# An SSM scan beside a SwiGLU block: the last feature tile's column halves in one stretch, and a layernorm moved ahead

## The chip, the cores and the metric

The kernel runs on one core of a Trainium2 chip. The metric is the device time of one execution in microseconds (us). The engines are called by their names: TensorE (PE in the profile; its weight loads are PEld), VectorE (DVE), ScalarE (ACT), GpSimd (POOL) and SyncE (SP), whose queue starts most of the DMAs.

## The reference, cut to what matters

The input x has 2048 rows (tokens) of 512 columns in bfloat16. The weights of the SwiGLU block have 1376 features. The output is the sum of x, a diagonal state space model and the SwiGLU block, both on the layernorm of x:

```python
xn = layernorm(x)                               # over the 512 columns
# state space model: 512 complex states, a recurrence over the 2048 tokens
h_t = Lam_bar * h_(t-1) + B_bar @ xn_t
y   = 2 * real(C @ h_t) + xn * Dskip
# SwiGLU
f   = (silu(xn @ w_gate) * (xn @ w_up)) @ w_down
out = x + y + f
```

## The kernel before

**Chunks.** The tokens are cut into four chunks of 512, and each chunk into four tiles of 128. `xnT` holds the transposed layernorm of all chunks. For a chunk c three stages run on TensorE: `gateup_chunk(c)` makes the products with `w_gate` and `w_up`, `bproj_chunk(c)` makes those with B (L357), and `out_chunk(c)` makes the output. `out_chunk(c)` first runs `out_ffn` for its four tiles: for each, one PSUM bank is opened and the contractions with `w_down` over the feature tiles are added into it (L513). It then runs `out_ssm` for the four tiles, which adds eight contractions of the scanned states with the matrix CF (L522) and closes the bank. The bank leaves through ScalarE (L529) and a DMA of GpSimd's queue that adds to the output in DRAM (L530); for the last chunk it leaves through VectorE. A PSUM bank holds 128x512 floats, and there are eight.

**Order of the stages.** TensorE runs, after a hand-written head: the gate of chunk 0 in two parts with bproj(0) between them, bproj(1), gate(1), bproj(2), out(0), gate(2), bproj(3), out(1), gate(3), out(2), out(3). Instructions are issued on each engine in the order in which the program's text emits them.

**The features.** 1376 features make ten tiles of 128 and a last one of 96. The gate stage begins with the last one. Its 96 gate columns and the last 32 of its up columns are put side by side into one weight tile `w_last`, so one group of four matmuls serves both (L458). The 64 up columns that are left (`wu_last`, L468) are half a weight tile. For two chunks they run as pairs of halves, 128x64 each, into the two halves of one bank's partitions. Chunks 0 and 1 have theirs in gate(1), and chunks 2 and 3 have theirs in gate(3). The results are copied by ScalarE into `ul` (L471) and multiplied by VectorE into `gu_last` (L473), of which there are two, one for even and one for odd chunks. `out_ffn` reads `gu_last` in its eleventh contraction.

**The backlog.** The work of VectorE for the state space model stands in a list, `backlog`, of entries with a cost and a tag. `pump(us)` lets as many of them out as the TensorE time that was just issued pays for; `need(tag)` lets everything out up to the last entry of that tag; `multiply(keep)` lets out the products of the gate stage (L451, L473), which stand in a list of their own. For a chunk the entries are: six rotation steps on `u` (L367, L377, L381), eight scans (L399), the carry (L408 to L413), six rotation steps back into `wt`. CF itself is made by eight entries (tag "cf"): ScalarE scales a column block into `cm` (L340, three buffers) and VectorE combines it (L343).

**The layernorms.** Those of chunks 2 and 3 go through the backlog too. `ln_rest` gives four statistics (L185, L186), the variance (L194) with GpSimd's power for the reciprocal root (L195), one VectorE entry for the bias (`nb`, L198), and four entries that normalize a tile on ScalarE (L208) and start its transposing DMA on SP's queue (L234). `spread` puts a list of entries one by one between those of another. Chunk 2's layernorm stands among chunk 0's scans; chunk 3's stands among chunk 1's scans. SP's queue also starts one DMA that copies x into the output (L734), before which no accumulating DMA may run.

Of the kernel before, what the change touches and what calls it, by code (L numbers as in the profile page):

```python
# [11 lines left out]
BF16 = mybir.dt.bfloat16  # L12
ALU = mybir.AluOpType
ACT = mybir.ActivationFunctionType
# [9 lines left out]
def kernel(  # L24
# [17 lines left out]
    nc = tc.nc  # L42
    _, L, D = A_x.shape
# [3 lines left out]
    CW = 512  # L47
    HW = CW // 2
    NT = L // 128
    NCH = L // CW  # L50
    TPC = CW // 128
    KD = D // 128
    NQ = Pst // 128
    FT = (F + 127) // 128
# [4 lines left out]
    LA, LB = 32, 64  # L59
# [4 lines left out]
    const = ctx.enter_context(tc.tile_pool(name="const", bufs=1))  # L64
    ssm = ctx.enter_context(tc.tile_pool(name="ssm", bufs=1))
    gut = ctx.enter_context(tc.tile_pool(name="gut", bufs=2))
    up_p = ctx.enter_context(tc.tile_pool(name="up_p", bufs=4))
    opool = ctx.enter_context(tc.tile_pool(name="opool", bufs=6))
# [4 lines left out]
    def bank(shape=(128, CW), dtype=F32):  # L73
        return psum.tile(list(shape), dtype, name="ps")
# [5 lines left out]
    out_v = out[0].rearrange("(n p) d -> p n d", p=128)  # L80
# [5 lines left out]
    xnT = const.tile([128, KD, L], BF16, name="xnT")  # L86
# [8 lines left out]
    wu_last = const.tile([128, KD, LB], BF16, name="wu_last")  # L95
    wd_sb = const.tile([128, FT, D], BF16, name="wd_sb")
# [5 lines left out]
    CF = const.tile([128, 2, NQ, D], BF16, name="CF")  # L102
# [62 lines left out]

    gu_last = [const.tile([128, CW], BF16, name=f"gu_last{i}") for i in range(2)]
    for t in (gu_last[0][LB + LA:128, :], gu_last[1][LB + LA:128, :], wd_sb[LB + LA:128, FT - 1, :]):
        nc.vector.memset(t, 0.0)  # L170


# [11 lines left out]
    def ln_stats(n):  # L184
        nc.vector.bn_stats(out=stats[:, n, :], in_=xall[:, n, :])  # L185
        nc.vector.bn_aggr(out=mv[:, n, :], in_=stats[:, n, :])  # L186
# [6 lines left out]
    def ln_rstd(a, b):  # L193
        nc.vector.tensor_scalar(out=ve[:, a:b], in0=mv[:, a:b, 1], scalar1=EPS, scalar2=None, op0=ALU.add)  # L194
        nc.gpsimd.tensor_tensor(out=rstd[:, a:b], in0=ve[:, a:b], in1=neg_half[:, 0:b - a], op=ALU.pow)  # L195

    def ln_nb(a, b):
        nc.vector.scalar_tensor_tensor(out=nb[:, a:b], in0=mv[:, a:b, 0], scalar=-1.0, in1=rstd[:, a:b],  # L198
                                       op0=ALU.mult, op1=ALU.mult)
# [32 lines left out]
    def xT_dma(n):  # L232
        c, i = divmod(n, TPC)
        nc.sync.dma_start_transpose(out=xnT[:, :, n * 128:(n + 1) * 128], in_=xn_tile(c)[:, i, :])  # L234
# [12 lines left out]
    V = nc.vector  # L247
# [177 lines left out]
    gu_tiles = {}  # L425
    u_pair = {}
    products = []
# [24 lines left out]

    up_last = {}

    def gateup_last(c):
        ps = bank()
        for k in range(KD):
            nc.tensor.matmul(ps[:], lhsT=w_last[:, k, :], rhs=xnT[:, k, c * CW:(c + 1) * CW],  # L458
                             start=(k == 0), stop=(k == KD - 1))
        u = up_last[c] = up_p.tile([128, CW], BF16, name="ul", bufs=2)  # L460
        nc.scalar.activation(out=gu_last[c % 2][0:LB + LA, :], in_=ps[0:LB + LA], func=ACT.Silu)
        nc.scalar.copy(out=u[LB:LB + LA, :], in_=ps[LB + LA:128])
        if c % 2 == 0:
            return
        ps = bank()
        for k in range(KD):
            for i in range(2):
                nc.tensor.matmul(ps[i * LB:(i + 1) * LB], lhsT=wu_last[:, k, :],  # L468
                                 rhs=xnT[:, k, (c - 1 + i) * CW:(c + i) * CW], start=(k == 0), stop=(k == KD - 1))
        for i in range(2):  # L470
            nc.scalar.copy(out=up_last[c - 1 + i][0:LB, :], in_=ps[i * LB:(i + 1) * LB])  # L471
            g, u = gu_last[(c - 1 + i) % 2][0:LB + LA, :], up_last[c - 1 + i][0:LB + LA, :]
            products.append(lambda g=g, u=u: V.tensor_tensor(out=g, in0=g, in1=u, op=ALU.mult))  # L473

    def gateup_tile(c, fi):
        if fi == FT - 1:
# [22 lines left out]
    o_tiles = {}  # L499

    def out_blocks(n):

        return ((0, D // 2), (D // 2, D - 128), (D - 128, D)) if n == NT - 1 else ((0, D),)

    def out_ffn(n):
        c, i = divmod(n, TPC)
        o_tiles[n] = []
        for lo, hi in out_blocks(n):
            o = bank((128, hi - lo))
            o_tiles[n].append(o)  # L510
            for fi in range(FT):
                t = gu_last[c % 2] if fi == FT - 1 else gu_tiles[c][:, fi, :]
                nc.tensor.matmul(o[:], lhsT=t[:, i * 128:(i + 1) * 128], rhs=wd_sb[:, fi, lo:hi],  # L513
                                 start=(fi == 0), stop=False)

    def out_ssm(n):
        c, i = divmod(n, TPC)
        res = opool.tile([128, D], BF16, name="res")
        for o, (lo, hi) in zip(o_tiles[n], out_blocks(n)):
            for part in range(2):  # L520
                for q in range(NQ):
                    nc.tensor.matmul(o[:], lhsT=w_tiles[c][:, part, q, i * 128:(i + 1) * 128],  # L522
                                     rhs=CF[:, part, q, lo:hi], start=False, stop=(part == 1 and q == NQ - 1))
            if c == NCH - 1:
                V.tensor_tensor(out=res[:, lo:hi], in0=o[:], in1=xn_end[:, i, lo:hi], op=ALU.add)  # L525
                for a, b in ((0, D // 2), (D // 2, D)) if i == 0 else ((lo, hi),):
                    (nc.sync if b == D else nc.scalar).dma_start(out=out_v[:, n, a:b], in_=res[:, a:b])
            else:
                nc.scalar.copy(out=res[:, lo:hi], in_=o[:])  # L529
                nc.gpsimd.dma_start(out=out_v[:, n, lo:hi], in_=res[:, lo:hi], accum_op=ALU.add)  # L530

# [4 lines left out]
    def queue(tag, ops, at=None):  # L538
        ops = [[op[0], op[1], op[2] if len(op) > 2 else None, tag] for op in ops]
        if at is None:  # L540
            backlog.extend(ops)
        else:
            backlog[at:at] = ops

    def step():
        for item in backlog[0:AHEAD + 1]:
            if item[2] is not None:
                item[2]()
                item[2] = None
        cost, op, _, _ = backlog.pop(0)  # L550
        op()
        owed[0] -= cost

    def pump(us):

        owed[0] += us
        while backlog and owed[0] >= backlog[0][0] * 0.5:
            step()
        if not backlog:
            owed[0] = 0.0  # L560

    def multiply(keep):

        while len(products) > keep:
            products.pop(0)()
            owed[0] -= 0.65

    def need(tag):

        while any(item[3] == tag for item in backlog):  # L570
            step()
# [12 lines left out]
    def ln_rest(c, on_act):  # L584
        ops = [(0.7, lambda n=n: ln_stats(n)) for n in range(c * TPC, (c + 1) * TPC)]
        def fin():
            ln_rstd(c * TPC, (c + 1) * TPC)
        def nbf():
            ln_nb(c * TPC, (c + 1) * TPC)
        ops += [(0.1, fin)]  # L590
        tail = [(0.1, nbf)] if on_act else []
        for n in range(c * TPC, (c + 1) * TPC):
            def one(n=n):
                (norm_act if on_act else norm_dve)(n)
                xT_dma(n)
            tail.append((0.05 if on_act else 0.35, one))
        return ops, tail
# [70 lines left out]
    def gateup_chunk(c):  # L668
        for fi in [FT - 1, *range(FT - 1)]:
            gateup_tile(c, fi)  # L670
            pump(GU)
            multiply(1)

    def out_chunk(c):

        multiply(0)
        for n in range(c * TPC, (c + 1) * TPC):
            out_ffn(n)
            pump(FT * 0.2163)
        need(f"ssm{c}")  # L680
        need("cf")
        for n in range(c * TPC, (c + 1) * TPC):
            out_ssm(n)
            pump(2 * NQ * 0.2163)

    def spread(ops, others, tag, tag2):

        others = list(others)
        for op in ops:
            queue(tag, [op])  # L690
            if others:
                queue(tag2, [others.pop(0)])

    def queue_ssm(c):
        fwd, back = ssm_ops(c)
# [12 lines left out]
    fwd0, back0 = ssm_ops(0)  # L708
    stats2, norm2 = ln_rest(2, True)
    queue("ssm0", fwd0[0:2] + [(1.5, params_b)] + fwd0[2:6])  # L710
    queue("ln2", stats2)
    queue("ssm0", fwd0[6:8])
    spread(fwd0[8:] + back0, norm2, "ssm0", "ln2")
    queue("cf", c_ops())
    load_late()
    for fi in range(G0, FT):
# [6 lines left out]

    bproj_chunk(1)
    fwd1, back1 = ssm_ops(1)
    stats3, norm3 = ln_rest(3, True)
    queue("ssm1", fwd1[0:6])
    queue("ln3", stats3)
    queue("ssm1", fwd1[6:8])
    spread(fwd1[8:] + back1, norm3, "ssm1", "ln3")  # L730
    gateup_chunk(1)
    nc.gpsimd.dma_start(out=dsk_bc[:], in_=A_Dskip.partition_broadcast(128))
    bproj_chunk(2)
# [44 lines left out]
```

## Time and profile before

| what | value |
|---|---|
| time, median of 3 runs | 179.62 us (179.45 to 179.9) |
| the profiled execution's own time | 179.41 us |
| its span in the profile | 177.6 us |
| TensorE busy | 172.7 us |
| VectorE busy | 154.2 us |
| ScalarE busy | 94.3 us |
| DMA traffic | 15.53 MB |
| granted TensorE clock | 1.0 |

The span runs from the first to the last instruction that the profile has; the execution's own time is 1.8 us longer. In a row of the timeline stand the start in us from the span's start, the duration in us, the engine, the line, the operation, the tiles and shapes, the number of instructions that were merged into the row, and in brackets the engine's idle time just before, with what ended it. Matmuls are pipelined: the duration of one is longer than the distance between the starts of two.

### The profile page before, as it was taken

The page shows a single profiled execution, that of the slowest core. Times are in us where ns is not written, and L with a number is a line of the kernel's source. Part 1 is how long each engine was busy: PE and PEld are TensorE (multiplying, and loading weights), DVE is VectorE, ACT ScalarE, POOL GpSimd, SP SyncE. Part 2 cuts the span into 40 slices and gives each one's busy share as a digit, 9 for nine tenths or more (in the row PEclk, how much of TensorE's full clock was granted, in tenths as well). Part 3 has the DMA queues.
Part 4 walks back from the last instruction along what each step waited for, and adds up shares of the span by engine and source line. Part 5 has one row for each costly group of instructions (what it writes and reads, how often), then busy time and mean ns, then how long its engine had stood idle before and what let it go on. Part 6 is the DMA issues. An engine that isn't in the chain of part 4 may idle for free.

```text
span 177.6 us, 2450 instructions
## 1 busy us (share of the span) xinstructions
PE 172.7 (97%) x900; PEld 83.1 (47%) x916; DVE 154.2 (87%) x237; ACT 94.3 (53%) x173; POOL 23.2 (13%) x29
## 2 busy tenths in 40 slices
PE   8999999999999999999999999999999999999993
PEld 2784444444444444444444444444444444444743
DVE  6789997999999999999999999999999999940033
ACT  4589696978499965033997660024866600220000
POOL 6003000001300000029000000013505000150000
PEclk9999999999999999999999999999999999999999
DMA  5998948993146400022820000007276900072012
GB/s 157 320 265 234 146 95 232 350 140 89 30 87 208 181 0 0 0 30 29 122 61 0 0 0 0 4 2 85 30 119 94 147 0 0 0 87 32 4 49 69
DMA packets 29131, 15.53 MB, mean 87 GB/s; under 512 B 18848, under 2 KB 29056, under 8 KB 29088
## 3 DMA queue, kind: packets, MB, share of 16 engines
q1 hardware_dynamic: 24416, 11.41, 28.3%
q0 software_dynamic: 3456, 3.28, 13.9%
q10 hardware_dynamic: 1248, 0.69, 1.4%
q8 instruction: 7, 0.11, 0.3%
q14 instruction: 4, 0.03, 0.1%
HBM read 8.03 MB, written 5.24 MB: 75 GB/s over the span
## 4 chain that ended last, share of the span: by engine, by line
PE 95%; DVE 1%; DMA 1%; issue 1%
PE ps L432 36%; PE ps L513 21%; PE ps L357 15%; PE ps L522 15%; PE ps L605 3%; PE ps L458 2%; DMA xall<-in_A_x_dram 1%; PE ps L468 1%; PE ps L220 1%; DVE stats L185 0%; DVE stats L612 0%; DVE xall L203 0%; DVE res L525 0%; PE ps L582 0%; DVE mv L186 0%
## 5 line engine op out<-in xcount | busy, mean ns | idle before, releaser
L432 PE MATMUL ps<-xnT,wg 128*128 128x512 bf16 x143 | 37.6, 379 | 0.3
L432 PE MATMUL ps<-xnT,wu 128*128 128x512 bf16 x146 | 37.5, 379 | 0.1
L513 PE MATMUL ps<-wd_sb,guT 128*128 128x512 bf16 (+2 forms) x177 | 37.2, 355 | 0.2
L399 DVE TENSOR_TENSOR_SCAN g<-r_t,car,u 128x512 bf16<-128x512 f32 x24 | 28.9, 1266 | 0.0
L522 PE MATMUL ps<-CF,wt 128*128 128x512 bf16 (+2 forms) x140 | 28.1, 355 | 0.2
L357 PE MATMUL ps<-xnT,BT 128*128 128x512 bf16 x126 | 28.2, 379 | 0.1
L529 ACT CAST res<-ps 128x512 bf16<-128x512 f32 x12 | 7.0, 585 | 38.4 <-PE ps L522 38.4
L446 ACT ACTIVATE guT<-ps 128x512 bf16<-128x512 f32 x40 | 24.8, 620 | 3.8 <-PE ps L432 3.7
L447 ACT CAST u<-ps 128x512 bf16<-128x512 f32 x40 | 24.2, 604 | 4.1 <-PE ps L432 4.0
L513 PEld LDWEIGHTS <-guT 128*128 128x128 bf16 x180 | 16.9, 98 | 18.0
L432 PEld LDWEIGHTS <-wu 128*128 128x128 bf16 x148 | 14.5, 98 | 17.5
L432 PEld LDWEIGHTS <-wg 128*128 128x128 bf16 x148 | 14.3, 98 | 17.6 <-issue 0.8
L530 POOL DMA_DIRECT2D out_dram<-res x12 | 11.1, 998 | 87.2 <-ACT res L529 87.2
L522 PEld LDWEIGHTS <-wt 128*128 128x128 bf16 x144 | 13.5, 98 | 14.2
L357 PEld LDWEIGHTS <-BT 128*128 128x128 bf16 x128 | 12.5, 98 | 15.1
L359 ACT CAST u<-ps 128x512 bf16<-128x512 f32 x32 | 17.5, 589 | 3.1 <-PE ps L357 3.0
L525 DVE TENSOR_TENSOR res<-ps,xn_end 128x512 bf16<-128x512 f32 (+2 forms) x6 | 3.0, 514 | 14.5 <-PE ps L522 14.5
L451 DVE TENSOR_TENSOR guT<-guT,u 128x1024 bf16<-128x1024 bf16 x20 | 13.5, 680 | 0.0
L367 DVE TENSOR_TENSOR pm<-u,c 128x2048 bf16<-128x2048 bf16 x8 | 9.8, 1221 | 1.2 <-ACT c L284 1.1
L195 POOL TENSOR_TENSOR rstd<-ve,neg_half 128x4 f32<-128x4 f32 x3 | 5.2, 1749 | 40.2 <-DVE ve L194 40.2
L185 DVE BATCH_NORM_STATS2 stats<-xall 128x6 f32<-128x512 bf16 x14 | 9.4, 671 | 1.1 <-DMA xall<-in_A_x_dram 1.1
L367 DVE TENSOR_TENSOR pm<-g,c 128x2048 bf16<-128x2048 bf16 x8 | 9.7, 1218 | 0.1
(108 smaller groups left out, 166.1 us busy)
## 6 DMA issues: line engine op xcount, KB each, us to landing
out_dram<-in_A_x_dram SPq DMA_DIRECT2D x1, 1536.0 KB, 8.9
out_dram<-res POOLq DMA_DIRECT2D x12, 128.0 KB, 3.1
out_dram<-xall POOLq DMA_DIRECT2D x3, 512.0 KB, 5.7
wd_sb<-in_B_w_down_dram SPq DMA_DIRECT2D x1, 1280.0 KB, 10.3
xall<-in_A_x_dram SPq DMA_DIRECT2D x1, 1024.0 KB, 6.3
xall<-in_A_x_dram SPq DMA_DIRECT2D x2, 256.0 KB, 4.6
wg<-in_B_w_gate_dram SPq DMA_DIRECT2D x1, 512.0 KB, 5.2
wu<-in_B_w_up_dram SPq DMA_DIRECT2D x1, 512.0 KB, 6.1
```

The source lines that it names most:

```text
L185: nc.vector.bn_stats(out=stats[:, n, :], in_=xall[:, n, :])
L357: nc.tensor.matmul(ps[:], lhsT=BT[:, part, k, q * 128:(q + 1) * 128], rhs=xnT[:, k, c * CW:(c + 1) * CW], start=(k == 0), stop=(k == KD - 1))
L359: nc.scalar.copy(out=u_tiles[c][:, part, q, :], in_=ps[:])
L367: V.tensor_tensor(out=t[:], in0=flat(src()[:, i]), in1=flat(tab[:]), op=ALU.mult)
L399: V.tensor_tensor_scan(out=g()[:, part, q, :], data0=r_t[:, q:q + 1].to_broadcast([128, CW]), data1=u_tiles[c][:, part, q, :], initial=ini ...
L432: nc.tensor.matmul(ps[:fs, lo:hi], lhsT=wslice(groups, fi, k), rhs=xnT[:, k, c * CW + lo:c * CW + hi], start=(k == 0), stop=(k == KD - 1))
L446: nc.scalar.activation(out=guT[:fs, fi, :], in_=psg[:fs], func=ACT.Silu)
L447: nc.scalar.copy(out=u_pair[c][:fs, fi % 2, :], in_=psu[:fs])
L451: products.append(lambda: V.tensor_tensor(out=g, in0=g, in1=u, op=ALU.mult))
L513: nc.tensor.matmul(o[:], lhsT=t[:, i * 128:(i + 1) * 128], rhs=wd_sb[:, fi, lo:hi], start=(fi == 0), stop=False)
L522: nc.tensor.matmul(o[:], lhsT=w_tiles[c][:, part, q, i * 128:(i + 1) * 128], rhs=CF[:, part, q, lo:hi], start=False, stop=(part == 1 and q ...
L530: nc.gpsimd.dma_start(out=out_v[:, n, lo:hi], in_=res[:, lo:hi], accum_op=ALU.add)
```

## The change

It does four things.

- All 16 column halves of the last feature tile, of all four chunks, run in one stretch (`up_halves`) in `out_chunk(0)`, behind the down projection and ahead of `out_ssm`. The copies into `ul` (four buffers) follow them on ScalarE. There are three `gu_last` tiles, and chunk c uses number c mod 3.
- Chunk 0's contraction with its `gu_last` leaves `out_ffn`. Its four banks stay open through `out_ssm(0)`, and `out_end(0)` adds that contraction, closes the banks and lets them leave; it stands in gate(2), behind feature tile 0. Each bank leaves with one copy and one DMA, as before.
- Because the stretch reads chunk 3's `xnT`, chunk 3's layernorm leaves chunk 1's scans and stands, behind chunk 2's, among the scans and back rotation of chunk 0, ahead of the entries that make CF.
- `spread` takes one tag for each entry, and what is left of the second list follows at its end.

On SP's queue the four transposes of chunk 3 come to stand ahead of the copy of x into the output, and on GpSimd the third power comes to stand ahead of the load of `dsk_bc`.

```diff
-    gu_last = [const.tile([128, CW], BF16, name=f"gu_last{i}") for i in range(2)]
+    gu_last = [const.tile([128, CW], BF16, name=f"gu_last{i}") for i in range(3)]
...
+    def product_last(c):
+        g, u = gu_last[c % 3][0:LB + LA, :], ul(c)[0:LB + LA, :]
+        products.append(lambda: V.tensor_tensor(out=g, in0=g, in1=u, op=ALU.mult))
+
+    def up_halves():
+        pss = []
+        for c in range(0, NCH, 2):
+            ps = bank()
+            pss.append(ps)
+            for k in range(KD):
+                for i in range(2):
+                    nc.tensor.matmul(ps[i * LB:(i + 1) * LB], lhsT=wu_last[:, k, :],
+                                     rhs=xnT[:, k, (c + i) * CW:(c + i + 1) * CW], start=(k == 0), stop=(k == KD - 1))
+        for c in range(NCH):
+            i = c % 2
+            nc.scalar.copy(out=ul(c)[0:LB, :], in_=pss[c // 2][i * LB:(i + 1) * LB])
+        product_last(0)
+        product_last(1)
...
-            for fi in range(FT):
-                t = gu_last[c % 2] if fi == FT - 1 else gu_tiles[c][:, fi, :]
-                nc.tensor.matmul(o[:], lhsT=t[:, i * 128:(i + 1) * 128], rhs=wd_sb[:, fi, lo:hi],
+            for fi in range(FT - 1):
+                nc.tensor.matmul(o[:], lhsT=gu_tiles[c][:, fi, i * 128:(i + 1) * 128], rhs=wd_sb[:, fi, lo:hi],
                                  start=(fi == 0), stop=False)
+            if c > 0:
+                out_last(n, o, lo, hi, False)
...
     def gateup_chunk(c):
         for fi in [FT - 1, *range(FT - 1)]:
             gateup_tile(c, fi)
             pump(GU)
             multiply(1)
+            if c == 2 and fi == 0:
+                out_end(0)
...
             out_ffn(n)
             pump(FT * 0.2163)
+        if c == 0:
+            need("ln3")
+            up_halves()
+            multiply(0)
         need(f"ssm{c}")
         need("cf")
...
+    def out_end(c):
+        for n in range(c * TPC, (c + 1) * TPC):
+            o = o_tiles[n][0]
+            out_last(n, o, 0, D, True)
+            out_leave(n, o, opool.tile([128, D], BF16, name="res"))
...
+    stats3, norm3 = ln_rest(3, True)
     queue("ln2", stats2)
     queue("ssm0", fwd0[6:8])
-    spread(fwd0[8:] + back0, norm2, "ssm0", "ln2")
+    spread(fwd0[8:] + back0, norm2 + stats3 + norm3, "ssm0",
+           ["ln2"] * len(norm2) + ["ln3"] * (len(stats3) + len(norm3)))
     queue("cf", c_ops())
...
-    stats3, norm3 = ln_rest(3, True)
-    queue("ssm1", fwd1[0:6])
-    queue("ln3", stats3)
-    queue("ssm1", fwd1[6:8])
-    spread(fwd1[8:] + back1, norm3, "ssm1", "ln3")
+    queue("ssm1", fwd1 + back1)
     gateup_chunk(1)
```

More of the change, by code (lines that the diff above doesn't have):

```diff
@@ L164 @@
     nc.gpsimd.iota(out=jidx[:], pattern=[[1, CW]], base=0, channel_multiplier=0, allow_small_or_imprecise_dtypes=True)
-    gu_last = [const.tile([128, CW], BF16, name=f"gu_last{i}") for i in range(2)]
-    for t in (gu_last[0][LB + LA:128, :], gu_last[1][LB + LA:128, :], wd_sb[LB + LA:128, FT - 1, :]):
+    gu_last = [const.tile([128, CW], BF16, name=f"gu_last{i}") for i in range(3)]
+    for t in (*(g[LB + LA:128, :] for g in gu_last), wd_sb[LB + LA:128, FT - 1, :]):
         nc.vector.memset(t, 0.0)
@@ L453, with ul @@
     up_last = {}
+    def ul(c):
+        if c not in up_last:
+            up_last[c] = up_p.tile([128, CW], BF16, name="ul", bufs=4)
+        return up_last[c]
+    def product_last(c):
[15 more added lines that the diff above has]
+        product_last(1)
     def gateup_last(c):
@@ L459, in gateup_last @@
                              start=(k == 0), stop=(k == KD - 1))
-        u = up_last[c] = up_p.tile([128, CW], BF16, name="ul", bufs=2)
-        nc.scalar.activation(out=gu_last[c % 2][0:LB + LA, :], in_=ps[0:LB + LA], func=ACT.Silu)
+        u = ul(c)
+        nc.scalar.activation(out=gu_last[c % 3][0:LB + LA, :], in_=ps[0:LB + LA], func=ACT.Silu)
         nc.scalar.copy(out=u[LB:LB + LA, :], in_=ps[LB + LA:128])
[L463 to L473, printed above, removed]
+        if c > 1:
+            product_last(c)
     def gateup_tile(c, fi):
@@ L510, in out_ffn, with out_last @@
             o_tiles[n].append(o)
-            for fi in range(FT):
-                t = gu_last[c % 2] if fi == FT - 1 else gu_tiles[c][:, fi, :]
-                nc.tensor.matmul(o[:], lhsT=t[:, i * 128:(i + 1) * 128], rhs=wd_sb[:, fi, lo:hi],
+            for fi in range(FT - 1):
+                nc.tensor.matmul(o[:], lhsT=gu_tiles[c][:, fi, i * 128:(i + 1) * 128], rhs=wd_sb[:, fi, lo:hi],
                                  start=(fi == 0), stop=False)
+            if c > 0:
+                out_last(n, o, lo, hi, False)
+    def out_last(n, o, lo, hi, stop):
+        c, i = divmod(n, TPC)
+        nc.tensor.matmul(o[:], lhsT=gu_last[c % 3][:, i * 128:(i + 1) * 128], rhs=wd_sb[:, FT - 1, lo:hi],
+                         start=False, stop=stop)
     def out_ssm(n):
         c, i = divmod(n, TPC)
-        res = opool.tile([128, D], BF16, name="res")
+        if c > 0:
+            res = opool.tile([128, D], BF16, name="res")
         for o, (lo, hi) in zip(o_tiles[n], out_blocks(n)):
@@ L522, in out_ssm @@
                     nc.tensor.matmul(o[:], lhsT=w_tiles[c][:, part, q, i * 128:(i + 1) * 128],
-                                     rhs=CF[:, part, q, lo:hi], start=False, stop=(part == 1 and q == NQ - 1))
+                                     rhs=CF[:, part, q, lo:hi], start=False, stop=(c > 0 and part == 1 and q == NQ - 1))
             if c == NCH - 1:
@@ L527, in out_ssm, with out_leave @@
                     (nc.sync if b == D else nc.scalar).dma_start(out=out_v[:, n, a:b], in_=res[:, a:b])
-            else:
-                nc.scalar.copy(out=res[:, lo:hi], in_=o[:])
-                nc.gpsimd.dma_start(out=out_v[:, n, lo:hi], in_=res[:, lo:hi], accum_op=ALU.add)
+            elif c > 0:
+                out_leave(n, o, res)
+    def out_leave(n, o, res):
+        nc.scalar.copy(out=res[:], in_=o[:])
+        nc.gpsimd.dma_start(out=out_v[:, n, :], in_=res[:], accum_op=ALU.add)
     backlog = []
@@ L684, in out_chunk, with spread @@
             pump(2 * NQ * 0.2163)
-    def spread(ops, others, tag, tag2):
-        others = list(others)
+    def out_end(c):
[3 more added lines that the diff above has]
+            out_leave(n, o, opool.tile([128, D], BF16, name="res"))
+    def spread(ops, others, tag, tags):
+        others = list(zip(others, tags))
         for op in ops:
@@ L691, in spread @@
             if others:
-                queue(tag2, [others.pop(0)])
+                op, t = others.pop(0)
+                queue(t, [op])
+        for op, t in others:
+            queue(t, [op])
     def queue_ssm(c):
```

## The prediction

> **What bounds the kernel now.** The page first, its spans and the shares of the chain that ended last:
>
> ```profile
> span 177.6 us, 2450 instructions
> PE 172.7 (97%) x900; PEld 83.1 (47%) x916; DVE 154.2 (87%) x237; ACT 94.3 (53%) x173; POOL 23.2 (13%) x29
> PE 95%; DVE 1%; DMA 1%; issue 1%
> ```
>
> TensorE is busy for 97% and carries 95% of the chain: a change gains only what shortens TensorE's own row of matmuls, and loses only where TensorE is made to wait. Second, TensorE's timeline around the column halves (L468), in chunk 1's and in chunk 3's gate stage:
>
> ```profile
> 38.52 1.03 PE L458 MATMUL ps<-xnT,w_last 128*128 128x512 bf16 x4
> 39.48 1.05 PE L468 MATMUL ps<-xnT,wu_last 128*64 128x512 bf16 x8
> 40.47 1.04 PE L432 MATMUL ps<-xnT,wg 128*128 128x512 bf16 x4
> ...
> 122.49 1.03 PE L458 MATMUL ps<-xnT,w_last 128*128 128x512 bf16 x4
> ...
> 124.44 1.04 PE L432 MATMUL ps<-xnT,wg 128*128 128x512 bf16 x4
> ```
>
> Third, the weight loads of the same place, then the border between the down projection and the SSM contraction of chunk 0:
>
> ```profile
> 39.48 0.57 PEld L468 LDWEIGHTS <-wu_last 128*64 128x64 bf16 x8 [0.42 <-issue]
> 40.46 0.55 PEld L432 LDWEIGHTS <-wg 128*128 128x128 bf16 x4 [0.41 <-issue]
> ```
> ```profile
> 73.93 0.38 PE L513 MATMUL ps<-wd_sb,gu_last 128*128 128x512 bf16 x1
> 74.15 3.18 PE L522 MATMUL ps<-CF,wt 128*128 128x512 bf16 x13
> ```
>
> One matmul lasts 0.38, four last 1.03, so they start (1.03 - 0.38)/3 = 0.217 apart; I call that a slot. From the first L458 to the first L432 behind the halves there are 1.95 us both times. Four full matmuls and four pairs of halves fill 8 slots, 1.73. The 0.22 that is left is lost at the two borders between 128 and 64 columns.
>
> **The change on TensorE.** The number of matmuls is the same on every line. Two stretches of halves become one of 16, so two of four borders go: -0.22 us. The 4 contractions of chunk 0's last tile move from its down projection into chunk 2's gate: 0.87 earlier, 0.87 later, nothing in sum. Up to chunk 0's out_ssm the moves cancel: its predecessors lose 1.09 (the stretch in chunk 1) and 0.87, and gain 8 slots and two borders, 1.95. So out_ssm(0) is asked for at 74.15 as before, and the 0.22 is gained when chunk 3's gate no longer holds a stretch.
>
> **The weight loads against a rule.** The loader stands still for 0.42 and 0.41 around a stretch, but the matmuls cover most of it: by their starts only 0.22 is lost, and I take that. Were both idle times lost in full, a stretch would cost 0.83. The Trainium skill, TensorEngine Tiling (Array Packing), Key Properties, says that changing the tiling mode drains TensorE; by a drain of the loader's whole idle time the gain would be 0.83, and the matmul rows here bear out a quarter of that.
>
> **The layernorm that is moved.** This is where the change can lose. Chunk 3's four statistics, its rstd on GpSimd, four normalizations on ScalarE and four transposes on SP's queue now stand among chunk 0's scans and back rotation, ahead of the CF products that out_ssm(0) reads. The rows of VectorE before, in the old order and then the layernorm in its old place:
>
> ```profile
> 45.69 0.39 DVE L473 TENSOR_TENSOR gu_last<-gu_last,ul 96x512 bf16<-96x512 bf16 x1
> ...
> 49.44 0.39 DVE L473 TENSOR_TENSOR gu_last<-gu_last,ul 96x512 bf16<-96x512 bf16 x1
> ...
> 53.73 0.13 DVE L408 TENSOR_TENSOR ct<-g,cos 128x4 f32<-128x4 bf16 x1
> ...
> 54.26 1.22 DVE L367 TENSOR_TENSOR pm<-g,c 128x2048 bf16<-128x2048 bf16 x1
> 55.39 0.68 DVE L451 TENSOR_TENSOR guT<-guT,u 128x1024 bf16<-128x1024 bf16 x1
> 56.00 2.35 DVE L367 TENSOR_TENSOR pm<-g,s 128x2048 bf16<-128x2048 bf16 x2
> ...
> 58.87 1.22 DVE L377 TENSOR_TENSOR wt<-pm 128x2048 bf16<-128x2048 bf16 x1
> 60.12 1.22 DVE L367 TENSOR_TENSOR pm<-g,c 128x2048 bf16<-128x2048 bf16 x1
> ...
> 63.12 0.74 DVE L343 SCALAR_TENSOR_TENSOR CF<-CT,nc2im,cm 128x512 bf16<-128x512 bf16 x1
> ...
> 64.39 4.06 DVE L343 SCALAR_TENSOR_TENSOR CF<-CT,nc2im,cm 128x512 bf16<-128x512 bf16 x6
> ...
> 76.63 0.69 DVE L185 BATCH_NORM_STATS2 stats<-xall 128x6 f32<-128x512 bf16 x1
> ...
> 79.95 0.17 DVE L194 TENSOR_SCALAR ve<-mv 128x4 f32<-128x4 f32 x1
> ...
> 83.57 0.14 DVE L198 SCALAR_TENSOR_TENSOR nb<-mv,rstd 128x4 f32<-128x4 f32 x1
> ```
> ```profile
> 14.80 1.47 POOL L195 TENSOR_TENSOR rstd<-ve,neg_half 128x4 f32<-128x4 f32 x1 [10.52 <-DVE ve L194]
> ...
> 80.20 1.93 POOL L195 TENSOR_TENSOR rstd<-ve,neg_half 128x4 f32<-128x4 f32 x1 [2.34 <-DVE ve L194]
> ```
>
> VectorE runs without idle time in this stretch, so I add slots in the built order. The carry products (ct) stood at 53.73; two gu_last products of 0.39 leave from ahead of them: 52.95. From there to ve: four statistics (76.63 to 79.95, 3.32), ct (0.53), the first rotation product (1.13), two guT products (0.61 each), two more rotation products (2.35): 61.49. The power is done 2.18 after ve starts (80.20 + 1.93 - 79.95), so nb can run at 63.67. Only one L377 (1.25) stands between: VectorE now waits 0.9 for GpSimd, and ScalarE waits behind it with five of the eight evictions of bproj(2) in its queue. Those five and the first three output tiles hold all eight PSUM banks; the fourth tile is due ten slots ahead of the stretch, near 70.0, and the first two of the five are out by 65.6. Behind nb come two guT products, a rotation product and L381 (3.7 in all): the first CF could start at 67.4 in place of 63.12, and eight at (4.06 - 0.74)/5 = 0.66 would end at 72.8. But each CF needs a scaled copy (cm) from ScalarE:
>
> ```profile
> 65.17 0.72 ACT L340 ACTIVATE cm<-CT,c2re 128x512 f32<-128x512 bf16 x1
> 65.83 0.72 ACT L340 ACTIVATE cm<-CT,nc2re 128x512 f32<-128x512 bf16 x1
> 66.46 0.57 ACT L359 CAST u<-ps 128x512 bf16<-128x512 f32 x1
> 66.92 0.72 ACT L340 ACTIVATE cm<-CT,c2re 128x512 f32<-128x512 bf16 x1
> ...
> 83.74 0.81 ACT L208 ACTIVATE xn_end<-xall,nb,rstd 128x512 bf16<-128x512 bf16 x1 [1.91 <-DVE nb L198]
> 84.46 0.57 ACT L461 ACTIVATE gu_last<-ps 96x512 bf16<-96x512 f32 x1
> ```
>
> Slots on ScalarE: cm 0.65, eviction 0.46, normalization 0.72; the first normalization starts 0.17 behind nb, at 63.85. In the built order the eighth cm has 4 normalizations, 5 evictions and 7 cm ahead: 63.85 + 2.88 + 2.30 + 4.55 = 73.58, done at 74.30. So the seventh CF ends at 74.45 and the eighth at 75.1. out_ssm(0) reads the seventh (part 0, q 3) in its fourth matmul, 74.15 + 0.65 = 74.80, and the eighth in its last, 75.66. Margins: 0.35 and 0.56. The sum takes no stall; each us beyond 0.35 goes straight to the end.
>
> The power's price is the open term: 1.47 at 14.80, beside a tensor_scalar, 1.93 beside scans. Beside L377 it isn't shown. I take 1.93; held until L377 ends at 62.8, plus 1.47, it would be done at 64.3, 0.6 later, with a stall of 0.25; at 1.47 it would gain nothing, since no stall is there to shorten. The Trainium skill, SBUF — State Buffer, Who interferes with whom, says that a VectorE instruction with two SBUF inputs contends with a GpSimd one that reads SBUF and that the later one blocks; the two durations agree with it in direction, and by it the sum would be +0.03 in place of -0.22.
>
> **The other queues.** SP's rows before:
>
> ```profile
> 54.40 0.65 SPq L734 DMA_DIRECT2D out_dram<-in_A_x_dram  x1
> 84.58 5.71 SPq L234 DMA_TRANSPOSE xnT<-xn_end  x4
> ```
> ```profile
> out_dram<-in_A_x_dram SPq DMA_DIRECT2D x1, 1536.0 KB, 8.9
> xnT<-xn_end SPq DMA_TRANSPOSE x4, 2.9
> ```
>
> The fourth normalization ends at 63.85 + 3 x 0.72 + 2 x 0.46 + 2 x 0.65 + 0.81 = 69.0; its transpose lands 2.9 later, at 72. The stretch starts at 74.15 - 1.95 = 72.2 and reads chunk 3 in its second half, at 73.2: margin 1.2. The copy of x into the output, queued behind these transposes, goes out near 70.5 rather than 54.40 and lands near 79.4; the first accumulation into it now comes behind chunk 2's first gate tile, after 74.15 + 44 slots = 83.7. The first gu_last product stands behind six rotation steps after the last CF: 75.1 + 6 x 1.22 + 0.39 = 82.8, for a matmul at 83.7. If CF is late, TensorE is late by as much, and this margin stays. One more memset (a half of the two below) ends far inside the wait for x:
>
> ```profile
> 1.25 0.55 DVE L170 MEMSET gu_last<- 32x256 uint32 x2
> ...
> 2.81 0.69 DVE L185 BATCH_NORM_STATS2 stats<-xall 128x6 f32<-128x512 bf16 x1 [0.75 <-DMA xall<-in_A_x_dram]
> ```
>
> **Sum.** The profiled execution took 179.41 us, 1.8 of it outside the span; less 0.22 that is 179.19. The median of the runs is 179.62, 0.21 higher, so I forecast 179.62 - 0.22 = 179.40. A measurement of this kernel tells about 0.3%, 0.54 us, from no change: the forecast is a no-change.
>
> **Rivals.** (1) CF comes late, slower. Place: ScalarE's queue behind nb. Each full duration in place of a slot adds 4 x 0.09, 5 x 0.11 and 7 x 0.07, 1.4 in all, and a held power 0.6: 2.0 late, less the margin 0.35 a stall of 1.65, 181.05. For it: two chains of some ten and twenty us have to meet to within 0.35, and VectorE idles for GpSimd where it didn't before. Against it: ScalarE's rows show slots, not full durations, wherever it is behind. It undoes the gain when CF is 0.57 late, and is slower by the bound when 1.1 late; half the price, 1.0 late, gives 180.05. (2) The borders cost the loader's idle time, 0.83: 178.79, faster; against it the starts of the matmuls. (3) The 0.22 belongs to each pair of halves, not to the borders, and one stretch of 16 loses as much as two of 8: 179.62. Against it, the weight loads' two idle times stand at the borders alone.
>
> **Chances.** Forecast 0.48. Rival 1 0.42, of which 0.09 stays within the bound. Rival 2 0.07. Rival 3 0.03. Within 0.3%: 0.48 + 0.09 + 0.03 = 0.60; slower 0.33; faster 0.07. The range, 179.0 to 180.8, leaves out rival 2 and the upper end of rival 1; the forecast's own is 179.1 to 179.7.
>
> **What would show it.** Right: one stretch of 16 halves before the first out_ssm matmul, with 0.42 of idle weight loads at each end, no idle time of TensorE there, and chunk 3's gate without a gap. Wrong: a wait of TensorE for CF behind the stretch (rival 1), or for xnT inside it; nb on VectorE later than 64.3; a TensorE row that ends over 0.5 earlier (rival 2).

## The result and the profile after

| | before | after |
|---|---|---|
| median of 14 runs | 179.50 us (179.3 to 179.9) | 179.18 us (179.0 to 179.37) |
| the profiled execution | 179.41 us | 179.15 us |
| its span | 177.6 us | 177.3 us |

The ratio is 0.998, with a 95% interval of 0.9972 to 0.9988: the change takes 0.32 us (0.22 to 0.50). It is a gain, and it is smaller than the 0.54 us that the prediction counts as a change. The forecast was -0.22 us, at 179.40. The median of before moved from 179.62 to 179.50 with more runs, so 0.12 of the distance between 179.40 and 179.18 is the starting point's.

The page of the changed kernel, its span and its chain by engine:

```profile
span 177.3 us, 2449 instructions
PE 98%; issue 1%; DVE 0%
```

TensorE's timeline there, from the down projection of chunk 0 to chunk 2's gate, and the weight loads around the stretch:

```profile
63.53 8.80 PE L528 MATMUL ps<-wd_sb,guT 128*128 128x512 bf16 x39
72.26 1.92 PE L472 MATMUL ps<-xnT,wu_last 128*64 128x512 bf16 x16
74.11 7.08 PE L545 MATMUL ps<-CF,wt 128*128 128x512 bf16 x31
81.03 1.03 PE L483 MATMUL ps<-xnT,w_last 128*128 128x512 bf16 x4
...
83.62 1.03 PE L535 MATMUL ps<-wd_sb,gu_last 128*128 128x512 bf16 x4
```
```profile
72.26 1.44 PEld L472 LDWEIGHTS <-wu_last 128*64 128x64 bf16 x16 [0.42 <-issue]
74.11 1.84 PEld L545 LDWEIGHTS <-wt 128*128 128x128 bf16 x10 [0.41 <-issue]
```

One stretch, with the same two idle times of the loader at its ends as each of the two stretches had before, and no idle time of TensorE in any of these rows. out_ssm(0) starts at 74.11, where it started at 74.15. Chunk 3's gate holds no stretch any more:

```profile
123.33 1.03 PE L483 MATMUL ps<-xnT,w_last 128*128 128x512 bf16 x4
124.19 1.03 PE L432 MATMUL ps<-xnT,wg 128*128 128x512 bf16 x4
```

Its first L432 starts at 124.19, 0.25 earlier than the 124.44 of before. Of that, 0.04 was there at out_ssm(0); the other 0.21 is gained in between. VectorE, GpSimd, ScalarE and SP's queue, in this order, at the moved layernorm and at CF, and the landings of SP's transfers:

```profile
61.30 0.16 DVE L194 TENSOR_SCALAR ve<-mv 128x4 f32<-128x4 f32 x1
61.41 1.23 DVE L377 TENSOR_TENSOR wt<-pm 128x2048 bf16<-128x2048 bf16 x1
63.54 0.16 DVE L198 SCALAR_TENSOR_TENSOR nb<-mv,rstd 128x4 f32<-128x4 f32 x1 [0.90 <-POOL rstd L195]
...
67.09 0.74 DVE L343 SCALAR_TENSOR_TENSOR CF<-CT,nc2im,cm 128x512 bf16<-128x512 bf16 x1
...
72.77 2.08 DVE L343 SCALAR_TENSOR_TENSOR CF<-CT,nc2im,cm 128x512 bf16<-128x512 bf16 x3 [0.34 <-ACT cm L340]
...
81.95 0.75 DVE L462 TENSOR_TENSOR gu_last<-gu_last,ul 96x512 bf16<-96x512 bf16 x2
```
```profile
61.54 1.97 POOL L195 TENSOR_TENSOR rstd<-ve,neg_half 128x4 f32<-128x4 f32 x1 [16.10 <-DVE ve L194]
```
```profile
63.74 0.81 ACT L208 ACTIVATE xn_end<-xall,nb,rstd 128x512 bf16<-128x512 bf16 x1 [3.74 <-DVE nb L198]
...
73.24 0.72 ACT L340 ACTIVATE cm<-CT,nc2re 128x512 f32<-128x512 bf16 x1
```
```profile
64.58 5.49 SPq L234 DMA_TRANSPOSE xnT<-xn_end  x4
70.11 0.65 SPq L774 DMA_DIRECT2D out_dram<-in_A_x_dram  x1
```
```profile
out_dram<-in_A_x_dram SPq DMA_DIRECT2D x1, 1536.0 KB, 7.0
...
xnT<-xn_end SPq DMA_TRANSPOSE x4, 2.4
```

The last three CF products share a row; they start (2.08 - 0.75)/2 = 0.67 apart, so the seventh ends at 74.18 and the eighth at 74.85. The matmuls that read them start at 74.11 + 0.65 = 74.76 and 75.62. The margins are 0.58 and 0.77.

### The profile page after: what moved, and what is told of

It is laid out like the page before. It is cut to its first block, busy times and chain, and to the rows that moved or that the text cites. A ratio compares the mean times of both kernels' runs of the same rounds, so it can differ in the third digit from the quotient of the medians.

```text
span 177.3 us, 2449 instructions
## 1 busy us (share of the span) xinstructions
PE 172.9 (97%) x900; PEld 83.6 (47%) x916; DVE 154.4 (87%) x238; ACT 94.7 (53%) x173; POOL 23.2 (13%) x29
## 4 chain that ended last, share of the span: by engine, by line
PE 98%; issue 1%; DVE 0%
PE ps L432 36%; PE ps L528 19%; PE ps L545 16%; PE ps L357 16%; PE ps L631 3%; PE ps L608 2%; PE ps L483 2%; PE ps L535 2%; PE ps L472 1%; PE ps L220 1%; DVE res L548 0%; PE ps L250 0%
## 5 line engine op out<-in xcount | busy, mean ns | idle before, releaser
L432 PE MATMUL ps<-xnT,wg 128*128 128x512 bf16 x144 | 37.8, 379 | 0.4
L432 PE MATMUL ps<-xnT,wu 128*128 128x512 bf16 x145 | 37.3, 379 | 0.0
L528 PE MATMUL ps<-wd_sb,guT 128*128 128x512 bf16 (+2 forms) x177 | 36.7, 355 | 0.2
L432 PEld LDWEIGHTS <-wu 128*128 128x128 bf16 x148 | 14.5, 98 | 17.5
L432 PEld LDWEIGHTS <-wg 128*128 128x128 bf16 x148 | 14.4, 98 | 17.2
L556 POOL DMA_DIRECT2D out_dram<-res x12 | 10.5, 1041 | 78.0 <-ACT res L555 78.0
```

The lines of the kernel that those rows point to most:

```text
L432: nc.tensor.matmul(ps[:fs, lo:hi], lhsT=wslice(groups, fi, k), rhs=xnT[:, k, c * CW + lo:c * CW + hi], start=(k == 0), stop=(k == KD - 1))
L528: nc.tensor.matmul(o[:], lhsT=gu_tiles[c][:, fi, i * 128:(i + 1) * 128], rhs=wd_sb[:, fi, lo:hi], start=(fi == 0), stop=False)
L556: nc.gpsimd.dma_start(out=out_v[:, n, :], in_=res[:], accum_op=ALU.add)
```

## The experiments

Times are medians of 4 to 12 runs, or single runs where that is said. Ratios are to the kernel before, run on the same chip; it took 179.41 and 179.40 us there, in place of 179.50. The changed kernel was not timed again beside the experiments, so a difference to its 179.18 is uncertain by about the 0.1 that the kernel before moved. What each execution loses by itself is read from the traces at the end of this section.

**Two stretches.** The halves of the changed kernel are cut in two again, inside the fourth output tile's down projection. Chunk 3's layernorm is let out ahead of that tile.

```diff
+    half_at = {4: [(0, k) for k in range(4)], 9: [(1, k) for k in range(4)]}
...
             for fi in range(FT - 1):
                 nc.tensor.matmul(o[:], ...)
+                if n == TPC - 1:
+                    for p, k in half_at.get(fi, ()):
+                        half_step(p, k)
```

> The changed kernel with its 16 column halves cut into two stretches again: the four pairs of chunks 0 and 1 stand in the middle of the fourth output tile's down projection (behind feature tile 4), those of chunks 2 and 3 behind its tile 9. All else as in the changed kernel. Border theory (0.22 us for each stretch of halves, whatever its length): two more borders than in the changed kernel, 179.18 + 0.22 = 179.40, as good as the kernel before (179.50). Rival, the 0.22 belongs to each group of four pairs: 179.18. Rival, the loader's idle time of 0.83 a stretch is lost in full: 180.0.

Measured: 179.39 us, ratio 1.0001 (0.999 to 1.0012). With the borders back, the gain is gone, though the layernorm, the deferred contraction and the order of the other engines stay as in the changed kernel. TensorE's timeline:

```profile
71.22 1.05 PE L521 MATMUL ps<-xnT,wu_last 128*64 128x512 bf16 x8
72.21 1.25 PE L531 MATMUL ps<-wd_sb,guT 128*128 128x512 bf16 x5
73.39 1.05 PE L521 MATMUL ps<-xnT,wu_last 128*64 128x512 bf16 x8
```

From one stretch to the next it takes 73.39 - 71.22 = 2.17 for nine slots (1.95): 0.22 for a stretch.

**Eight stretches.** The same, one pair at a time.

```diff
+    half_at = {f + 1 + 4 * p: [(p, f)] for p in range(2) for f in range(4)}
```

> The same 16 halves as eight stretches of one pair each, one behind each of the feature tiles 1 to 8 of the fourth output tile's down projection. Border theory: seven stretches more, 7 x 0.22 = 1.54, 179.18 + 1.54 = 180.7. Rival, the cost belongs to the pairs: 179.2. Rival, the loader's idle time in full, 7 x 0.83 = 5.8: 185.0.

Measured: 180.74 us, ratio 1.0079 (1.0061 to 1.0098). TensorE's timeline of this kernel:

```profile
71.20 0.41 PE L521 MATMUL ps<-xnT,wu_last 128*64 128x512 bf16 x2
71.55 0.39 PE L531 MATMUL ps<-wd_sb,guT 128*128 128x512 bf16 x1
71.86 0.41 PE L521 MATMUL ps<-xnT,wu_last 128*64 128x512 bf16 x2
```

A pair and a full matmul are two slots, 0.43; from pair to pair it takes 71.86 - 71.20 = 0.66. So 0.23 is lost on each stretch, also where it holds a single pair. Two and eight stretches, timed together, take 179.39 and 180.74: 1.35/6 = 0.225 for each further one. The second costs 0.21 over the 179.18 of the changed kernel, or 0.38 by the two ratios, uncertain by some 0.25 to either side. Rivals 2 and 3 of the prediction are out. The loader's idle time is not even a fixed amount for each border; in this kernel it is 0.23 between the pairs:

```profile
70.88 0.10 PEld L531 LDWEIGHTS <-guT 128*128 128x128 bf16 x1 [0.23 <-issue]
71.20 0.11 PEld L521 LDWEIGHTS <-wu_last 128*64 128x64 bf16 x2 [0.23 <-issue]
```

**The layernorm's move alone**, in the kernel before.

```diff
-    spread(fwd0[8:] + back0, norm2, "ssm0", "ln2")
+    spread(fwd0[8:] + back0, norm2 + stats3 + norm3, "ssm0",
+           ["ln2"] * len(norm2) + ["ln3"] * (len(stats3) + len(norm3)))
...
-    queue("ssm1", fwd1[0:6])
-    queue("ln3", stats3)
...
+    queue("ssm1", fwd1 + back1)
```

> The kernel before with the layernorm's move alone: chunk 3's layernorm among chunk 0's scans and back rotation, the column halves and the last contraction where they were. Border theory: no border is saved and the margins of CF (0.58 us in the trace of the changed kernel) hold, so 179.5, as the kernel before. Rival, the gain comes from the move of the layernorm (a later stage of VectorE or ScalarE that becomes free): 179.2. Rival, CF is late here: over 179.5, with idle time of TensorE ahead of the fourth contraction of chunk 0.

Measured: 179.54 us, ratio 1.0006 (0.9995 to 1.0017). The move gains nothing, and nothing by it is seen to be lost: out_ssm(0) starts at 74.20 in its trace, without idle time. With the kernel of two stretches, this leaves the borders as what the change gains by. The rows of TensorE, VectorE and GpSimd:

```profile
74.20 2.10 PE L522 MATMUL ps<-CF,wt 128*128 128x512 bf16 x9
```
```profile
62.10 0.69 DVE L451 TENSOR_TENSOR guT<-guT,u 128x1024 bf16<-128x1024 bf16 x1
62.70 1.22 DVE L377 TENSOR_TENSOR wt<-pm 128x2048 bf16<-128x2048 bf16 x1
```
```profile
62.27 1.38 POOL L195 TENSOR_TENSOR rstd<-ve,neg_half 128x4 f32<-128x4 f32 x1 [16.76 <-DVE ve L194]
```

Here a guT product stands beside the power, which takes 1.38 in place of 1.97; the section on the prediction comes back to it.

**The deferred contraction at once.** `out_end(0)` stands directly behind `out_ssm` of chunk 0.

```diff
         for n in range(c * TPC, (c + 1) * TPC):
             out_ssm(n)
             pump(2 * NQ * 0.2163)
+        if c == 0:
+            out_end(0)
```

> The changed kernel with chunk 0's last contraction directly behind its state space contraction, in place of behind feature tile 0 of chunk 2's gate. In the changed kernel's trace TensorE is at that place at 81.03 us, and the product that it would read (the first gu_last product on VectorE) ends at 82.3. Theory: TensorE stands still for 1.3 us there, 179.18 + 1.3 = 180.5. Rival, the place costs nothing since VectorE brings the product earlier when TensorE asks earlier: 179.2.

Measured: 180.51 us, ratio 1.0064 (1.0047 to 1.0081), 1.33 over the changed kernel's 179.18. The waits of TensorE in this kernel name the product, and VectorE's row stands where it stood in the changed kernel (81.95):

```profile
PE ps L535 <- DVE gu_last L462: 1.2, 1, 1.2
```
```profile
81.94 0.75 DVE L462 TENSOR_TENSOR gu_last<-gu_last,ul 96x512 bf16<-96x512 bf16 x2
```

So the place in chunk 2's gate is what makes the deferral free: the product is ready at 82.3 and asked for at 83.62.

**More work in ScalarE's queue.** Normalizations into a tile that nobody reads stand directly ahead of the four that the change moved: one, then three.

```diff
+                for _ in range(1 if n == (NCH - 1) * TPC else 0):   # 3 in the second kernel
+                    nc.scalar.activation(out=scratch[:], in_=xall[:, n, :], func=ACT.Identity,
+                                         scale=rstd[:, n:n + 1], bias=nb[:, n:n + 1])
                 (norm_act if on_act else norm_dve)(n)
```

> The changed kernel with one more normalization on ScalarE (of chunk 3's first tile, into a tile that nobody reads), directly ahead of the four that the change moved. In the changed kernel's trace the seventh CF ends at 74.18 us, and the matmul that reads it starts at 74.11 + 3 x 0.217 = 74.76: a margin of 0.58. Theory (ScalarE's queue behind nb carries CF, and what goes over the margin goes to the end in full): one slot of 0.72 more, a stall of 0.14, 179.18 + 0.14 = 179.3. Rival, the chain has no margin: 179.9. Rival, VectorE and not ScalarE sets CF: 179.18.

> The same with three more normalizations. Theory: 3 x 0.72 = 2.16 later, less the margin of 0.58 a stall of 1.6, 180.8; part of it can show as a wait of the column halves for chunk 3's transposes, which move by as much (margin 1.9 there). Rival, no margin: 181.3. Rival, VectorE sets CF: 179.2.

Measured: one, 179.43 us, ratio 0.9999 (0.999 to 1.0008); three, 181.19 us, ratio 1.0095 (1.0081 to 1.0109). Of the kernel with one, TensorE's out_ssm and VectorE's last CF row:

```profile
74.30 5.07 PE L547 MATMUL ps<-CF,wt 128*128 128x512 bf16 x22
```
```profile
73.63 2.08 DVE L345 SCALAR_TENSOR_TENSOR CF<-CT,nc2im,cm 128x512 bf16<-128x512 bf16 x3 [0.34 <-ACT cm L342]
```

The seventh CF ends at 73.63 + 0.67 + 0.75 = 75.05, for a matmul that was due at 74.30 + 0.65 = 74.95: 0.1 late, and with the handover the matmul starts at 75.10, a stall of 0.15 where 0.14 was expected. The timed loss to the changed kernel, 0.25 by the medians, is larger than that; the intervals of the two ratios, each some 0.15 us to either side, cover the difference, and within the execution 0.14 is lost (the table below). Of the kernel with three, the waits of TensorE, its timeline, ScalarE's row of the three, and VectorE's last CF row:

```profile
PE ps L547 <- DVE CF L345: 1.0, 1, 1.0
...
PE ps L474 <- DMA xnT<-xn_end: 0.3, 1, 0.3
```
```profile
63.93 8.80 PE L530 MATMUL ps<-wd_sb,guT 128*128 128x512 bf16 x40
72.66 1.27 PE L474 MATMUL ps<-xnT,wu_last 128*64 128x512 bf16 x9
74.20 1.02 PE L474 MATMUL ps<-xnT,wu_last 128*64 128x512 bf16 x7 [0.27 <-DMA xnT<-xn_end]
75.15 0.82 PE L547 MATMUL ps<-CF,wt 128*128 128x512 bf16 x3
77.02 2.32 PE L547 MATMUL ps<-CF,wt 128*128 128x512 bf16 x10 [1.04 <-DVE CF L345]
```
```profile
64.11 2.51 ACT L623 ACTIVATE scratch<-xall,nb,rstd 128x512 bf16<-128x512 bf16 x3 [3.71 <-DVE nb L200]
66.53 0.80 ACT L210 ACTIVATE xn_end<-xall,nb,rstd 128x512 bf16<-128x512 bf16 x1
```
```profile
75.55 2.08 DVE L345 SCALAR_TENSOR_TENSOR CF<-CT,nc2im,cm 128x512 bf16<-128x512 bf16 x3 [0.34 <-ACT cm L342]
```

The three took 66.53 - 64.11 = 2.42, not 2.16: the second and the third start 0.85 behind the one before, where the normalizations into different tiles start 0.72 apart. The three write the same tile; that this is the reason is likely, and not shown. The stage starts at other times in the two executions, so I count from its first matmul. From the first contraction of chunk 0 to the matmul that reads the seventh CF it takes 77.02 - 63.93 = 13.09; in the changed kernel 74.76 - 63.53 = 11.23. The difference, 1.86, is 2.42 less the margin of 0.58 (1.84). Of it, 0.64 comes in the stretch of the halves, which waits for chunk 3's transposes (75.15 - 72.66 = 2.49 against 74.11 - 72.26 = 1.85), as expected, and the rest at CF.

**The layernorm left in its old place**, with all halves in one stretch (one run).

```diff
-    queue("ssm1", fwd1 + back1)
+    queue("ssm1", fwd1[0:6])
+    queue("ln3", stats3)
+    queue("ssm1", fwd1[6:8])
+    spread(fwd1[8:] + back1, norm3, "ssm1", ["ln3"] * len(norm3))
```

> The changed kernel with chunk 3's layernorm back in its old place, among chunk 1's scans, and the column halves of all chunks still in one stretch ahead of chunk 0's state space contraction. Theory: the second half of the stretch waits for chunk 3's transposes. In the kernel before nb ran at 83.57 and the last of the four normalizations ended near 89.0, with a landing 2.4 to 2.9 later, 91.7; the halves ask at 73.15: a stall of 18, about 197.5. Rival, VectorE brings the layernorm forward as soon as TensorE waits: under 185.

Measured: 198.32 us. The waits of TensorE, and the granted clock over the span:

```profile
PE ps L472 <- DMA xnT<-xn_end: 17.0, 1, 17.0
```
```profile
PEclk9999999999999998555999999999999999999999
```

In this order of the stages the merge can't be had without the move. The granted clock falls to a half in the slices of the long wait. Within the execution 19.1 us are lost (the table below), and 17.0 of them are this wait; the rest isn't taken apart here.

**The bias directly behind the variance** (one run).

```diff
+        def fin_nb():
+            fin()
+            nbf()
-        ops += [(0.1, fin)]
-        tail = [(0.1, nbf)] if on_act else []
+        ops += [(0.1, fin_nb if c == NCH - 1 else fin)]
+        tail = [(0.1, nbf)] if on_act and c < NCH - 1 else []
```

> The changed kernel with chunk 3's bias (nb) issued directly behind its variance (ve), ahead of the back rotation's L377. VectorE then stands still while GpSimd takes the power, and no instruction with two SBUF inputs runs beside it. In ScalarE's queue the first normalization then stands ahead of all eight evictions of bproj(2) in place of five. If the power is slower beside such an instruction (1.97 us beside L377, 1.47 beside a tensor_scalar): 1.47 here, nb at 63.05. If not: 1.9, nb at 63.5. Theory for TensorE: eight full banks leave none for the first output tile, asked for at 63.53; the first eviction ends 0.2 + 0.72 + 0.58 behind nb, at 64.5 or 65.0, so a stall of 1.0 or 1.5: 180.2 or 180.7. Rival, the margin of CF grows by the earlier nb and nothing else changes: 179.2.

Measured: 179.92 us. Its rows of GpSimd, VectorE and TensorE:

```profile
61.76 1.01 POOL L195 TENSOR_TENSOR rstd<-ve,neg_half 128x4 f32<-128x4 f32 x1 [16.09 <-DVE ve L194]
```
```profile
62.80 0.17 DVE L198 SCALAR_TENSOR_TENSOR nb<-mv,rstd 128x4 f32<-128x4 f32 x1 [1.12 <-POOL rstd L195]
62.88 1.22 DVE L377 TENSOR_TENSOR wt<-pm 128x2048 bf16<-128x2048 bf16 x1
```
```profile
56.88 7.07 PE L357 MATMUL ps<-xnT,BT 128*128 128x512 bf16 x32
64.34 8.79 PE L528 MATMUL ps<-wd_sb,guT 128*128 128x512 bf16 x40 [0.39 <-ACT u L359]
```

The power took 1.01 with VectorE idle, less than either expectation, and nb came 0.74 earlier than in the changed kernel. But the kernel is slower: the first normalization now stands ahead of all eight evictions, the eight banks are full, and the first output tile waits. It was due at 56.88 + 32 x 0.217 = 63.8 and began at 64.34, a stall of 0.5. The expectation named the place; its size of 1.0 was for a power of 1.47, and the power was 0.46 shorter. That is a single run, and its 0.7 over the changed kernel is more than this stall. The table shows where the remainder lies: this execution is 0.25 late before the chunks begin, and behind that point it loses 0.55.

**Within the executions.** The profiled executions differ already in the hand-written head. In the changed kernel the first full group of matmuls with `w_up` is this row:

```profile
12.60 1.03 PE L432 MATMUL ps<-xnT,wu 128*128 128x512 bf16 x4
```

From the start of this group to the start of the last matmul the traces give, in us:

| kernel | start of the group | from there to the last matmul | over the changed kernel | expected |
|---|---|---|---|---|
| before | 12.62 | 161.94 | 0.23 | 0.22 |
| changed | 12.60 | 161.71 | | |
| two stretches | 12.64 | 161.94 | 0.23 | 0.22 |
| eight stretches | 12.61 | 163.30 | 1.59 | 1.54 |
| the layernorm's move alone | 12.68 | 161.94 | 0.23 | 0.22 |
| the contraction at once | 12.59 | 163.11 | 1.40 | 1.3 |
| one normalization more | 12.78 | 161.85 | 0.14 | 0.14 |
| three normalizations more | 13.00 | 163.56 | 1.85 | 1.6 |
| the layernorm in its old place | 12.73 | 180.77 | 19.06 | 18 |
| the bias behind the variance | 12.85 | 162.26 | 0.55 | 1.0 or 1.5 |

Each is a single execution. The head alone puts up to 0.4 us between them, more than the gain of the change; behind it the three kernels with two stretches agree to 0.01.

## Why the prediction was right

**The borders.** The term that the forecast rests on was 0.22 for a stretch, worked out from the starts of the matmuls. The experiments give 0.225 by the time of two and eight stretches, and 0.22 and 0.23 by the rows, also for a stretch of one pair. Between the two profiled executions 0.26 is gone, 0.23 of it behind the head. The measured gain of 0.32 has 0.22 at the end of its interval. That another part of the change gains the last 0.1 isn't shown: the kernel with two stretches has all other parts, and it stands at a ratio of 1.0001. The Trainium skill, TensorEngine Tiling (Array Packing), Key Properties, says that changing the tiling mode drains TensorE. A loss at the borders alone fits that; no run shows what TensorE does there. A loss in the size of the loader's idle time (0.83 a stretch) was wrong: eight stretches would have taken 185.0.

**The cancelling moves.** out_ssm(0) was to be asked for at the same time as before: 74.11 against 74.15.

**The layernorm's chain.** By its steps:

| step | forecast | after |
|---|---|---|
| ve on VectorE | 61.49 | 61.30 |
| idle time of VectorE ahead of nb | 0.9 | 0.90 |
| nb | 63.67 | 63.54 |
| first normalization | 63.85 | 63.74 |
| start of the eighth cm | 73.58 | 73.24 |
| seventh CF done | 74.45 | 74.18 |
| eighth CF done | 75.1 | 74.85 |
| margins | 0.35, 0.56 | 0.58, 0.77 |

The whole chain came 0.1 to 0.3 earlier than worked out. On ScalarE the slots of cm were 0.61 to 0.62 in place of 0.65. On VectorE two readings went against each other: the two gu_last products were taken out at their durations of 0.39, where the rows behind them start 0.31 and 0.32 later, and two rotation products were added at 2.35, where the row behind them starts 2.27 later. The forecast of no stall was a near thing: the end of the seventh CF was 0.27 off, against a margin of 0.35. That the wait is one of ScalarE's queue, and that what exceeds the margin reaches the end in full, is shown by the kernels with one and three normalizations more, which lose 0.14 and 1.85 behind the head. Rival 1, the slower side, was 0.58 us away from its first effect and 0.8 from undoing the gain of the borders.

**The power.** I took 1.93, from a row beside scans; it took 1.97 beside L377. The other bound, held until L377 ends and then 1.47, would have given 64.3 for its end; it was done at 63.5, 0.87 behind L377's end at 62.64. The step that was off is the 1.47, which is no undisturbed duration: with VectorE idle the power takes 1.01. The Trainium skill, SBUF — State Buffer, Who interferes with whom, says that a VectorE instruction with two SBUF inputs contends with a GpSimd one that reads SBUF, and that issue order decides who blocks. The runs agree that the power, the later one, is held: 1.10 until L377 ends and 0.87 behind it against 1.01 alone. Beside the guT product of the kernel with the layernorm's move alone it ended 0.86 behind that product's end (62.79), and in the kernel before, at 80.20, 0.83 behind the end of a scan (81.30). So it was luck in part that 1.93 fitted: a scan there lasts 1.28 and L377 1.23, and what counts is when the instruction beside the power ends.

**The other queues.** The fourth normalization ends at 68.85 (forecast 69.0), and its transpose lands 2.4 later, near 71.3 (72). The copy of x follows at 70.11 (70.5) and lands 7.0 later, at 77.1 (79.4). The first gu_last product ends at 82.3 (82.8), its matmul is at 83.62 (83.7).

**Banks.** I counted eight full banks and found the fourth tile safe. It was; the kernel with the bias moved shows that three evictions ahead of the wait are what keeps the first tile safe too, which the prediction didn't price.

## What to carry to other kernels

Where TensorE runs matmuls without a gap, an excursion into another tile width costs its two borders (0.22 us here) whatever its length: gather what needs that width into one stretch. Price a step that is moved ahead by the queue that it joins, instruction by instruction, up to the first reader; here CF could have come 0.58 us later at no loss, and 0.8 us later before the gain of 0.22 was gone. And look at what a wait holds back in its own queue: an eviction that stands behind it keeps a PSUM bank, and a wait that ends earlier can still cost time if it begins earlier in the order.

## What the runs showed of the hardware

The power on 128x4 numbers took 1.01 us on GpSimd with VectorE idle. Where VectorE was in a scan or a tensor_tensor when it started, it ended 0.80 to 0.87 us behind the end of that instruction, and took 1.38 (a guT product), 1.85 and 1.93 (scans) or 1.97 (L377) in all. VectorE wasn't held by it: in the kernel with the layernorm's move alone L377 started while the power ran, and lasted 1.22, as elsewhere. Beside a tensor_scalar the power took 1.47, which I had read as its own duration. The two borders of a stretch of 128x64 tiles cost TensorE 0.22 to 0.23 us together. In the eight-stretch kernel that is 0.13 behind a pair (71.20 to 71.55, where a slot is 0.217) and 0.09 ahead of the next (71.55 to 71.86), while the loader stood still for 0.23 at each; at the ends of a long stretch it stood still for 0.41 to 0.42 and TensorE lost no more.
